# A fused attention and long-convolution kernel: the short convolution moves to diagonal matmuls, the second-level transforms to smaller tiles

## The chip, the core and the metric

The kernel runs on one core of one Trainium2 chip. The core has a matrix engine (PE; its weight loads are listed as PEld), a vector engine (DVE), a scalar engine (ACT), a general engine (POOL) and a queue engine (SP) that issues most of the DMA transfers. Each engine works through its own instructions in order and waits for the others by semaphores. SBUF is the on-chip memory of 128 partitions; PSUM is where PE leaves its sums, from which DVE or ACT must move them. The metric is the device time of one execution in microseconds; the time before is 234.24 us, the median of 3 runs (233.44 to 234.29).

## The reference

Two independent halves share the sequence length S = 2048 and the width D = 576, and their outputs lie side by side in one array of 2048 x 1152.

```python
# A: attention of 32 heads of 18 over 8 earlier positions, 2 apart
q, k, v = split(x @ wqkv)                       # wqkv: 576 x 1728
idx = pos[:, None] - 2 * arange(8)[None, :]     # masked where negative
attn = softmax(where(mask, einsum(q, k[idx]) * 18 ** -0.5, -1e9))
a = einsum(attn, v[idx]).reshape(S, D) @ wo
# B: a causal convolution of 4 taps, then one as long as the sequence, by channel
k_shift = sum over t of k_pad[t:t + S] * shift_k[:, 3 - t]
kv = k_shift * v
y = irfft(rfft(kv, 2 * S) * rfft(ssm_k, 2 * S))[:S] + kv * ssm_D
b = q * y
```

## The kernel before

The program is a list of steps written out by hand, the string ORDER; each item names a step, its arguments and, after a colon, which PSUM pool it takes (a or b) and which engine evacuates it (s is ACT, v is DVE; without a letter the step's own default). Each pool has two buffers. Every engine, SP's queue included, gets its instructions in the order of this list, so the list decides what stands in front of what.

Half A. `xt` transposes x into xT, `qk`, `qt` and `v` project it (L381, L427, L402), v goes to DRAM (Dv). `lm` multiplies q with shifted k on DVE (L519, L524), `lb` sums over each head on PE (L530 to L540), `at` transposes logits so that positions lie on partitions, `sm` is the softmax in twelve small DVE and ACT steps, `bt` transposes the weights back, `vl` loads shifted copies of v from Dv, `pm` multiplies weights with them on DVE (L642), `ps` sums on PE (L658, L668), `po` applies wo (L680, L682) and stores.

Half B. The positions are split as 128 x 16. `cv` is the short convolution on DVE: for each of four groups of positions, four multiplications by a tap (L484), three additions (L486) and the multiplication by v (L488), each on 128x2304 elements. `sk` spreads the taps over partitions by matmuls. The long convolution is a Fourier transform in two levels. Level one is `sx` for kv and, after `lkn` has loaded ssm_k and `kt` has transposed it, `kp` for the kernel (both in `s1_part`, L456), which store to DRAM (Dx, Dk; L463). Level two loads the results in another arrangement (`xl`, `kl`; L600), multiplies by a table W2 (`xs`, `ks`; the function `s2`, L594), `gp` is the product of the spectra on DVE (L615, L616), `gi` the inverse of level two with the table IAt (L629), which stores to Dy (L634). `yl` loads Dy and q, `ys` is the last level and the product with q (L702, L706), which stores.

SBUF is full: areas r1 to r10 are used several times. Two of these shares matter here: ssm_k (`knats`) is loaded into the area of xT, so `lkn` waits until the last projection has read xT; and `vsr`, where level one is collected before it is stored, has two slots.

Tile positions: a matmul whose weights have 64 or 32 columns or rows uses a part of the PE array. Before, `s2` has weights of 128 rows x 64 columns (two positions), `g_inv` of 64 rows x 128 columns (two positions), `l_sum` and `p_sum` of 128 rows x 32 columns (four positions).

Transfers of level two: `by_rt` arranges Dx, Dk or Dy so that one DMA of 128 partitions x 2304 elements (8 rows of 288, contiguous in DRAM) holds one of eight groups. `v_load` is one DMA for 128 partitions, ordered head first and shift second.

Of the kernel before, what the change touches and what calls it, by code (L numbers as in the profile page):

```python
# [10 lines left out]
ALU = mybir.AluOpType  # L11
# [7 lines left out]
lx.0 tj lx.1 lx.2 lwq.1 lwv wm.11 tv t0 xt.0.2:av sk:b lk.0 t2 xt.1.2:av lwq.0 xt.1.0:av xt.1.1:bv xt.0.0:s xt.0.1:bv  # L19
xt.2.1:s qk.1.1.1:bs xt.2.2:s t3 tw t1 lx.3 cv.0.0:a lv.1 lk.1 qk.1.1.0:bs cv.0.1:b cv.0.2:b cv.0.3:b qk.1.0.0:s  # L20
xt.2.0:as lv.0 v.0.1:b cv.0.4:b v.1.1:bs wt lk.3 v.0.0:a xt.3.0:s cv.0.5:b lk.2 cv.0.6:a cv.0.7:b cv.1.0 qk.0.1.0:b
xt.3.1:b t4 xt.3.2:as cv.1.1 lm.0.1 cv.1.2:b t5 cv.1.3:b qk.0.0.0:a sx.0.0:s qt.1:s cv.1.4:a lm.0.0 v.2.1:as lv.2
sx.1.0:a cv.1.5 cv.1.6 sx.0.1:b qt.0:b sx.0.2:a cv.1.7:a qk.0.1.1 sx.1.1 qk.0.1.3:b v.0.2:s v.1.2:bs lm.0.2 v.1.0:a
sx.1.2:b qk.1.0.1:bs sx.3.0:b cv.2.0:a qk.0.0.1:a v.3.1:a cv.2.1 sx.3.1 sx.2.0:s cv.2.2:a qt.3:as v.2.0:as qk.1.1.3:bs
sx.2.1:s cv.2.3:a lm.1.0 lb.0:a cv.2.4 cv.2.5:b v.2.2:bs cv.2.6 lm.1.1 v.3.2:av sx.2.2:b sx.3.2:b lv.3 cv.2.7:b
qk.0.1.2:a lb.1:b cv.3.0:b lm.2.2 cv.3.1 cv.3.2:b v.3.0:a qk.1.1.2:bs lm.2.1 qk.0.0.3:bs qk.1.0.3:bs lwo sx.4.0:a
cv.3.3:a lm.3.1 qt.2 sx.4.1:b sx.4.2 qk.0.0.2:as cv.3.4:b cv.3.5:b sx.5.0:b lm.2.0 qk.1.0.2 sx.5.1:a lb.2:bs cv.3.6
cv.3.7:a lm.6.0 at.0.0 lkn sx.5.2:av lm.4.2 ia:b lm.3.0 sx.6.0:as sx.6.1:as sx.6.2:s kt.3:b sx.7.0 sx.7.1:a sx.7.2:av
kt.1:bv lb.3:bs kp.1.0:bs kp.1.1:as lm.4.1 lm.4.0 kp.1.2:bs kp.3.0:s kt.0:as kp.3.1:b kp.3.2:s lm.6.2 kt.2:av lb.4:a
kp.0.0 kp.0.1:s lm.6.1 at.0.1 sm.0.0 xl.0 kp.0.2 kp.2.0:av lm.5.1 kp.2.1:s kp.2.2:bs kt.5:as kt.4:s sm.0.1 lb.6:a  # L30
kp.5.0:av kp.5.1:bs lm.5.0 sm.0.2 xl.1 kp.5.2:as kp.4.0:bs kt.6 kp.4.1:a kp.4.2:as sm.0.3 kt.7:s lb.5:s kp.6.0:as
xs.0.0:bv kp.6.1:a xl.2 kp.6.2:as kp.7.0:v kp.7.1:a kp.7.2 lm.7.0 sm.0.4 lm.7.1 xs.1.0:as sm.0.5 xs.0.1 xs.1.1:a
sm.0.6 lb.7:bs sm.0.7 kl.1 sm.0.8 kl.0 kl.3 ks.1.0:s sm.0.9 sm.0.11 sm.0.10 ks.1.1:as ks.0.0 gp.1.0 at.1.0:av vl.0.0
gp.1.1 bt.0.1:v ks.0.1:bs gp.0.0 ks.3.0:bs gi.1.0:as vl.0.1 xs.2.0:b xl.4 xs.2.1:as gp.0.1 xl.3 bt.0.0:bv at.1.1:b
vl.1.2 sm.1.0 ks.3.1:as kl.2 gi.1.1 pm.0.0 gi.0.0:s xs.3.0:a sm.1.1 vl.0.2 ks.2.0:b pm.0.1 xs.3.1:as sm.1.2 gp.3.0
vl.1.0 kl.4 sm.1.3 gi.0.1:bs gp.3.1 pm.0.2 xs.4.0:as gp.2.0 ks.2.1:b ps.0.0:a pm.0.3 sm.1.4 ks.4.0:b xl.7 gp.2.1 kl.7
gi.3.0:a ks.4.1:b gp.4.0 xs.4.1:as vl.1.1 gi.2.0:s pm.1.4 ks.7.0:a xl.5 pm.1.0 ps.0.1:bs ks.7.1:s vl.2.0 gp.4.1 pm.1.1
xs.5.0:as sm.1.5 sm.1.6 xs.7.0:b kl.6 kl.5 gi.2.1:a xs.7.1:bs ps.1.0:v xs.5.1:b ks.5.0:a vl.3.0 xl.6 gi.4.0 ps.1.2:a
gi.3.1:s vl.3.2 pm.1.2 gi.4.1:as ks.5.1:s pm.0.4 sm.1.7 gp.5.0 pm.1.3 sm.1.8 ps.0.2:bs gp.5.1 xs.6.0 yl.3 sm.1.9 yl.2
ps.1.1:a ks.6.0:s po.0.0:s xs.6.1:bs sm.1.10 gi.5.0:a gp.7.0 yl.0 vl.2.1 gi.5.1:bs gp.6.0 po.0.2:a sm.1.11 vl.2.2  # L40
gp.7.1 po.0.1 ys.3.0:v ys.3.1:v yl.1 bt.1.1:as bt.1.0 po.0.3:bs ks.6.1:bs pm.2.0 gi.7.0:as gi.7.1 gp.6.1 pm.2.1
gi.6.0:a po.1.0:bs pm.2.2 ps.2.0:a vl.3.1 gi.6.1:bs pm.2.4 ys.2.0:av ps.2.2:bs pm.2.3 ys.0.0:v ys.2.1:bs ys.0.1:as
po.1.2 ps.2.1:a po.1.1:b po.1.3:bs pm.3.4 pm.3.0 po.2.0 yl.6 yl.4 pm.3.1 po.2.1:s ps.3.0:b pm.3.2 ps.3.2:a po.2.2:b
pm.3.3 ys.6.0:as yl.5 ys.1.0:v ys.1.1:v ps.3.1:as ys.6.1:v po.2.3:v yl.7 po.3.0:a ys.5.0:bv ys.5.1:a po.3.1:b po.3.2:s
ys.4.0:v po.3.3:b ys.4.1:v ys.7.0:a ys.7.1:bs
# [4 lines left out]
def kernel(  # L50
# [13 lines left out]
    nc = tc.nc  # L64
# [53 lines left out]
    def by_rt(Dd, dh, g):  # L118
        return Dd[dh].rearrange("r (l h) d -> (r l) h d", h=32)[:, 8 * g:8 * g + 8, :]
# [34 lines left out]
    class Ring:  # L154
# [21 lines left out]
    W2 = const.tile([128, 2, 32, 4, 16], BF16, name="W2")  # L176
    IAt = const.tile([128, 3, 16, 128], BF16, name="IAt")
# [6 lines left out]
    r1, r2, r3, r4, r5, r6, r7, r8, r9, r10 = (  # L184
        Area(f"area{i}", n) for i, n in enumerate((18528, 16384, 5 * S, 2560, 5 * 2 * D, 19 * D, 28 * D, 2 * S, 3168, 4 * D)))
    xns = [(r4 if i < 1 else r2).take(4, D) for i in range(4)]
    wq = r5.take(5, 2 * D)
# [4 lines left out]
    kfull = r6.take(19, D)  # L192
    vts = [r7.take(4, D) for _ in range(2)]
    tAr = Ring(r7.take(4, D), r7.take(4, D))
    skb = r7.take(4, D)
# [5 lines left out]
    for r in (r1, r3, r4, r5, r6, r7, r9, r10):  # L201
        r.reset()
    tB = r4.take(4, D)
    r4.reset()
# [17 lines left out]
    r7.reset(20 * D)  # L222
    shr = r7.take(4 * D)[0:1]
# [15 lines left out]
    def load_v(c):  # L239
        nc.sync.dma_start(vts[c % 2], vb16[:, 4 * c:4 * c + 4, :])  # L240

    def load_k(c):
        nc.sync.dma_start(kfull[:, 3 + 4 * c:7 + 4 * c, :], kb16[:, 4 * c:4 * c + 4, :])
        if c == 0:
            nc.sync.dma_start(kfull[1:113, 0:3, :], kb16[0:112, 13:16, :])
            nc.sync.dma_start(kfull[113:128, 0:3, :], kb16[112:127, 13:16, :])
# [31 lines left out]
    ones_f, ident_f, i4_f = mk.f32(128), mk.f32(128), mk.f32(32)  # L278
    junk, ones1 = mk.take(512), mk.take(128)[0:1]
    pib = const.tile([128, 1], FP32, name="pib")  # L280
    p_i, g1, n1 = mk.i32(1), mk.i32(128), mk.i32(2, 128)
    p_f, sc_f = mk.f32(1), mk.f32(8)
    g2, sc_i, n2, l_i = mk.i32(32, 16), mk.i32(4), mk.i32(2, 32, 16), mk.i32(4, 16)
    C2, lmask = mk.take(64, 16), mk.take(4, 16)
    ones_e, e_f = (mk.f32(HC + 2, H) for _ in range(2))

    def t_junk():
        nc.vector.memset(junk, 0.0)
        nc.vector.memset(pib[:], float(np.float32(np.pi)))
        nc.scalar.activation(sc_f[:, 0:1], pib[:], ACT.Sin, scale=0.0)  # L290
        nc.scalar.dma_start(shr, B_shift_k.rearrange("d j -> (d j)").unsqueeze(0))
# [18 lines left out]
    def t_padv():  # L310
        nc.vector.memset(kfull[0:1, 0:3, :], 0.0)
        nc.gpsimd.memset(row0[:], 0.0)
        nc.gpsimd.memset(row0[0:1, :], 1.0)
        nc.gpsimd.memset(ones1, 1.0)
# [10 lines left out]
    def t_second():  # L325
        nc.gpsimd.iota(g2, pattern=[[4, 32], [512, 16]], base=0, channel_multiplier=0)
        nc.gpsimd.iota(l_i, pattern=[[1, 4], [0, 16]], base=0, channel_multiplier=0)
        for i, bits in enumerate((3, 112, 4, 8)):
            nc.vector.tensor_single_scalar(sc_i[:, i:i + 1], p_i, bits, ALU.bitwise_and)
        nc.vector.tensor_copy(sc_f[:, 0:4], sc_i)  # L330
        t2f, s0 = sc_f[:, 4:5], sc_f[:, 5:6]
        nc.vector.tensor_scalar(t2f, sc_f[:, 1:2], 0.125, None, op0=ALU.mult)
        nc.vector.tensor_scalar(sc_f[:, 6:7], sc_f[:, 2:3], 0.25, None, op0=ALU.mult)
        nc.vector.tensor_tensor(t2f, t2f, sc_f[:, 6:7], ALU.add)
        nc.vector.tensor_scalar(s0, sc_f[:, 0:1], 128.0, 1.0, op0=ALU.mult, op1=ALU.add)
        nc.vector.tensor_tensor(s0, s0, t2f, ALU.mult)
        nc.vector.tensor_scalar(sc_f[:, 7:8], sc_f[:, 3:4], -256.0, 2048.0, op0=ALU.mult, op1=ALU.add)
# [5 lines left out]
        nc.vector.tensor_scalar(lmask, l_i, sc_f[:, 0:1], None, op0=ALU.is_equal)  # L343

    def t_w2():
        for i in range(2):
            nc.vector.tensor_tensor(W2[:, i], C2[:, 32 * i:32 * i + 32].unsqueeze(2).to_broadcast([128, 32, 4, 16]),
                                    lmask.unsqueeze(1).to_broadcast([128, 32, 4, 16]), ALU.mult)
# [61 lines left out]
    def v_load(c, k):  # L410
        nd = 8 if k < 2 else 2
        dst = (vSr if k < 2 else vStr).get((c, k))
        sl = Dv[D * c + 8 * k:D * c + 8 * k + 1, 2:3]
        nc.sync.dma_start(dst.rearrange("p d t -> p (d t)")[:, 0:nd * VT - 8],
                          bass.AP(tensor=sl.tensor, offset=sl.offset, ap=[[DH * VT, 32], [DIL, 4], [1, nd * VT - 8]]))
# [18 lines left out]
    def ia_tables():  # L434
        for zi in range(2):
            for p4 in range(2):
                ptr = psum("b", 2, 1024, dt=BF16)
                for v in range(8):
                    pr = 8 * p4 + v
                    nc.tensor.transpose(ptr[:, 0, 128 * v:128 * v + 128],  # L440
                                        W2[:, zi, 2 * pr:2 * pr + 2].rearrange("p h l f -> p (h l f)"), ident[:])
# [313 lines left out]
```

## Time and profile before

| Quantity | Value |
|---|---|
| median of 3 runs | 234.24 us |
| span of the profiled execution | 233.3 us |
| PE busy, instructions | 196.2 us, 1727 |
| DVE busy, instructions | 200.7 us, 199 |
| ACT busy, instructions | 164.7 us, 241 |
| POOL busy | 22.2 us |
| moved by DMA | 60.57 MB, mean 260 GB/s |

The profiled execution's own time is its span, 233.3 us: the trace holds nothing of the program outside it. That is 0.9 us under the median of the runs and just under the fastest.

A row of groups gives a line, the engine, the operation, what it writes and reads with the shape, how often, the busy time, the mean duration of one in ns, and the idle time of the engine before it. A matmul's duration contains the way through the array, so neighbours overlap: the rate of a series is read from its whole length. A row of stretches gives the busy time of each engine in a stretch with the number of instructions, then the granted clock of PE as a share, the share of time in which the DMA engines had packets (it can pass 1 where packets overlap) and the rate in GB/s.

### The profile page before, as it was taken

Reading aid. Unit: us, or ns where it says so; the run is one execution under the profiler, and the core shown is the slowest. Engines: PE = TensorE matmul, PEld = TensorE weight load, DVE = VectorE, ACT = ScalarE, POOL = GpSimd, SP = SyncE. Lnnn points to the kernel's source line nnn. Section 1 sums busy time; section 2 is a strip of 40 time slices with the busy share of each in tenths; the row PEclk is TensorE's granted clock in tenths of the full one; section 3 lists DMA queues with packets and bytes.
Section 4 is the critical chain, followed back from the end, with each engine's and each line's share of the span. In section 5 each row is a group of like instructions: output and inputs, shape, how many; then the busy total and the mean of one; then the engine's idle time right before and its main releaser. Section 6 shows DMA issues by size and latency. Waiting matters only on the chain. (4 is left out here: it accounts for less than half of the span.)

```text
span 233.3 us, 4423 instructions
## 1 busy us (share of the span) xinstructions
PE 196.2 (84%) x1727; PEld 112.5 (48%) x1736; DVE 200.7 (86%) x199; ACT 164.7 (71%) x241; POOL 22.2 (10%) x53
## 2 busy tenths in 40 slices
PE   7899969999999977959873979668898979896981
PEld 2644524544544444545532456434564656564661
DVE  2679999989596999778969999999999999996533
ACT  2675739677754969487989789899999758535321
POOL 8001540110210110200000000000000010010100
PEclk9999999999999996779998599999999999997999
DMA  6999823451169589977996998999798999799586
GB/s 221 348 276 393 248 85 106 155 162 48 55 198 268 134 273 327 218 221 211 307 290 207 330 353 326 374 355 400 306 360 299 327 332 379 274 275 339 121 272 214
DMA packets 46965, 60.57 MB, mean 260 GB/s; under 512 B 2368, under 2 KB 40064, under 8 KB 45920
## 3 DMA queue, kind: packets, MB, share of 16 engines
q1 hardware_dynamic: 46254, 57.78, 75.5%
q0 software_dynamic: 688, 2.51, 4.6%
q8 instruction: 13, 0.21, 0.4%
q14 instruction: 8, 0.07, 0.1%
q10 hardware_dynamic: 2, 0.00, 0.0%
HBM read 38.98 MB, written 21.31 MB: 258 GB/s over the span
## 5 line engine op out<-in xcount | busy, mean ns | idle before, releaser
L103 ACT ACTIVATE area<-psB 128x576 bf16<-128x576 f32 (+7 forms) x122 | 85.2, 745 | 32.2 <-PE psB L381 7.6
L103 ACT ACTIVATE area<-psA 128x576 bf16<-128x576 f32 (+7 forms) x105 | 75.6, 760 | 30.7 <-PE psA L381 12.0
L519 DVE TENSOR_TENSOR area<-area 128x4096 bf16<-128x4096 bf16 x16 | 36.4, 2285 | 5.7 <-PE psA L540 3.3
L642 DVE TENSOR_TENSOR area<-area,area 128x4096 bf16<-128x4096 bf16 (+1 forms) x20 | 40.7, 2069 | 0.1
L381 PEld LDWEIGHTS <-area 128*128 128x128 bf16 x160 | 15.5, 98 | 20.0 <-issue 3.0
L594 PEld LDWEIGHTS <-W 128*64 128x64 bf16 x256 | 14.1, 113 | 22.0 <-issue 15.0
L484 DVE TENSOR_TENSOR area<-area,area 128x2304 bf16<-128x2304 bf16 x16 | 21.6, 1362 | 0.8 <-PE psB L456 0.6
L594 PE MATMUL psB<-area,W 128*64 128x288 bf16 x160 | 16.2, 299 | 6.9 <-DMA area<-Dk 3.9
L381 PE MATMUL psB<-area,area 128*128 128x512 bf16 x85 | 20.1, 379 | 0.3
L693 POOL DMA_DIRECT2D area<-in_B_q_dram x8 | 6.0, 747 | 142.8 <-DVE area L706 119.2
L381 PE MATMUL psA<-area,area 128*128 128x512 bf16 x67 | 16.1, 379 | 2.7 <-DVE area L367 2.5
L456 PE MATMUL psB<-area,T 128*128 128x384 bf16 x58 | 14.8, 346 | 2.9 <-ACT area L103 2.7
L456 PEld LDWEIGHTS <-T 128*128 128x128 bf16 x96 | 9.3, 104 | 15.1 <-issue 9.2
L486 DVE TENSOR_TENSOR area<-area,area 128x2304 bf16<-128x2304 bf16 x12 | 16.3, 1356 | 0.3
L629 PEld LDWEIGHTS <-IAt 64*128 64x128 bf16 x256 | 12.4, 94 | 6.9 <-issue 4.0
L680 PEld LDWEIGHTS <-area 128*128 128x128 bf16 x128 | 12.4, 100 | 5.8 <-issue 2.6
L381 PE MATMUL psA<-area,wv 128*128 128x512 bf16 x60 | 13.9, 379 | 0.0
L594 PE MATMUL psA<-area,W 128*64 128x288 bf16 x96 | 10.2, 310 | 4.1 <-ACT area L103 3.6
L381 PEld LDWEIGHTS <-wv 128*128 128x128 bf16 x80 | 7.6, 98 | 9.4 <-issue 0.6
L616 DVE TENSOR_TENSOR area<-area 128x1152 bf16<-128x1152 bf16 x16 | 12.0, 749 | 0.0
L615 DVE TENSOR_TENSOR area<-area 128x1152 bf16<-128x1152 bf16 x16 | 11.9, 746 | 0.0
L456 PE MATMUL psA<-area,T 128*128 128x384 bf16 x38 | 10.0, 364 | 1.8 <-ACT area L103 1.7
(132 smaller groups left out, 270.1 us busy)
## 6 DMA issues: line engine op xcount, KB each, us to landing
area<-Dv SPq DMA_DIRECT2D x8, 1054.0 KB, 8.0
Dx<-area SPq DMA_DIRECT2D x16, 288.0 KB, 3.6
Dk<-area SPq DMA_DIRECT2D x16, 288.0 KB, 3.5
area<-Dx SPq DMA_DIRECT2D x8, 576.0 KB, 5.7
area<-Dk SPq DMA_DIRECT2D x8, 576.0 KB, 5.3
Dy<-area SPq DMA_DIRECT2D x8, 576.0 KB, 4.6
area<-Dy SPq DMA_DIRECT2D x8, 576.0 KB, 7.0
out_dram<-area SPq DMA_DIRECT2D x16, 288.0 KB, 3.7
```

Of the source, the lines that this page charges most:

```text
L103: nc.scalar.activation(dst, src, ACT.Copy, **({} if scale is None else {"scale": scale}))
L381: nc.tensor.matmul(ps[:, u, :], w[:, kb, cols[u]:cols[u] + 128], xT[:, kb, t], start=(kb == 0), stop=(kb == 4))
L456: nc.tensor.matmul(ps[:, ri, 0:384], T1[:, ri, :], sf[:, 384 * ch:384 * ch + 384], start=True, stop=not extra)
L484: nc.vector.tensor_tensor(tB if k else tA, kfull[:, 4 * c + 3 - j:4 * c + 7 - j, :], skb[:, j, :].unsqueeze(1).to_broadcast([128, 4, D]), ...
L486: nc.vector.tensor_tensor(tA, tA, tB, ALU.add)
L519: nc.vector.tensor_tensor(prr.get((n, h)), q2[h][:, :, 512 * aq:512 * aq + 512].unsqueeze(1).to_broadcast([128, 4, 2, 512]), kv, ALU.mult)
L594: nc.tensor.matmul(ps[64 * hp:64 * hp + 64, im, 0:HD], W2[:, im, 8 * g + 2 * prl + hp].rearrange("p l f -> p (l f)"), Wt[:, 2 * prl + hp, ...
L615: nc.vector.tensor_tensor(P[:, 0:2], X, K, ALU.mult)
L616: nc.vector.tensor_tensor(P[:, 2:4], X, swap, ALU.mult)
L629: nc.tensor.matmul(ps[:, hp, 0:HD], IAt[r, tab, 4 * g + 2 * hv + u, :], Pp[(i, hv)][r, n, u, :], start=(n == 0), stop=(n == 3), tile_posit ...
L642: nc.vector.tensor_tensor(P, vv, Lt[:, :, 512 * c:512 * c + 512].unsqueeze(2).to_broadcast([128, 2, nd, 512]), ALU.mult)
L680: nc.tensor.matmul(ps[:, di, 0:288], oT[:, 512 * ct + 128 * tt:512 * ct + 128 * tt + 128], wot[:, ct, d0:d1], start=(ct == 0), stop=False)
```

## The change

- `cv`: the rows of k are transposed on PE (`kx`, 80 transposes; with tokens along the free axis, kT). For each of 5 blocks of 128 channels and 2 halves of the 16 positions, 11 matmul steps use a slice of kT as weights (64 rows x 128 columns) and diagonal matrices of the taps (`dg`, built once on DVE) as the moving side; DVE then multiplies the sum in PSUM by v. `sk` and the multiplications and additions on DVE are gone.
- Level two: W2 has two instead of four interleaved blocks; `s2` uses weights of 64 rows x 32 columns (eight positions), `g_inv` of 32 rows x 64 columns (eight positions). There are twice as many of these matmuls, of the same free size 288. IAt is half as large, `ia` has three evacuations instead of six.
- Transfers: in the new arrangement the partitions of a group fall in two halves, so `xl`, `kl` and the store of `gi` are two DMAs of 64 partitions each; `vl` is four DMAs of 32 partitions each, ordered shift first and head second.
- `sm`: the reciprocal is written as bf16 at once, and the weights are normalised in place by one DVE operation per half instead of two that also reorder; `bt` reads them there.
- ORDER is a new list; several evacuations change engine.

```diff
-    def by_rt(Dd, dh, g):
-        return Dd[dh].rearrange("r (l h) d -> (r l) h d", h=32)[:, 8 * g:8 * g + 8, :]
+    def by_rt(Dd, dh, g, lg):
+        return Dd[dh].rearrange("r (k l h) d -> k r l h d", k=2, l=2)[lg, :, :, 8 * g:8 * g + 8, :]
...
     def v_load(c, k):
-        sl = Dv[D * c + 8 * k:D * c + 8 * k + 1, 2:3]
-        nc.sync.dma_start(dst.rearrange("p d t -> p (d t)")[:, 0:nd * VT - 8],
-                          bass.AP(tensor=sl.tensor, offset=sl.offset, ap=[[DH * VT, 32], [DIL, 4], [1, nd * VT - 8]]))
+        for j in range(4):
+            sl = Dv[D * c + 8 * k:D * c + 8 * k + 1, 2 + DIL * j:3 + DIL * j]
+            nc.sync.dma_start(dst.rearrange("p d t -> p (d t)")[32 * j:32 * j + 32, 0:nd * VT - 8],
+                              bass.AP(tensor=sl.tensor, offset=sl.offset, ap=[[DH * VT, 32], [1, nd * VT - 8]]))
...
-    def kv_conv(c, k):
-        tA = tAr.get(c) if k == 0 else tAr[c]
-        if k in (0, 1, 3, 5):
-            j = {0: 3, 1: 2, 3: 1, 5: 0}[k]
-            nc.vector.tensor_tensor(tB if k else tA, kfull[:, 4 * c + 3 - j:4 * c + 7 - j, :], skb[:, j, :].unsqueeze(1).to_broadcast([128, 4, D]), ALU.mult)
-        elif k < 7:
-            nc.vector.tensor_tensor(tA, tA, tB, ALU.add)
-        else:
-            nc.vector.tensor_tensor(tA, tA, vts[c % 2], ALU.mult)
+    def k_tok(c, h):
+        ptr = psum("b", 2, 1024, dt=BF16)
+        for u in range(2):
+            row = kas[c][:, 2 * h + u, :]
+            for cb in range(5):
+                c0 = min(128 * cb, D - 128)
+                nc.tensor.transpose(ptr[:, u, 128 * cb:128 * cb + 128], row[:, c0:c0 + 128], ident[:])
+        b0 = 4 * c + 2 * h
+        copy32(kT[:, :, b0:b0 + 2, 2:130], ptr[:, :, 0:640].rearrange("p u (k t) -> p k u t", k=5))
+
+    def kv_conv(cb, hb):
+        ps = psa()
+        lo = 8 * hb
+        order = (0, 4, -3, -2, -1, 1, 2, 3, 5, 6, 7)
+        for db in order:
+            b = lo + db
+            w0, w1 = max(b, lo), min(b + 4, lo + 8)
+            for u in range(2 if cb < 4 else 1):
+                hp = u if cb < 4 else 1
+                r = slice(64 * hp, 64 * hp + 64)
+                st = kT[r, cb, b % NT, 2:130] if b >= 0 else kT[r, cb, b % NT, 1:129]
+                nc.tensor.matmul(ps[:, u, 64 * (w0 - lo):64 * (w1 - lo)], st,
+                                 dg[r, cb, w0 - b:w1 - b, :].rearrange("p j c -> p (j c)"),
+                                 start=(db == order[0]), stop=(db == order[-1]), tile_position=(64 * hp, 0))
+        n = 2 if cb < 4 else 1
+        o = kv[:, lo:lo + 8, 128 * cb:128 * cb + 64 * n].rearrange("p b (u c) -> p u b c", u=n)
+        nc.vector.tensor_tensor(o, ps[:, 0:n].rearrange("p u (b c) -> p u b c", b=8), o, ALU.mult)
...
-    def s2(Wt, g, dst, h, scale):
-        for prl in (2 * h, 2 * h + 1):
+    def s2(Wt, g, dst, hh, scale):
+        for im in range(2):
             ps = psb()
-            for im in range(2):
-                for hp in range(2):
-                    nc.tensor.matmul(ps[64 * hp:64 * hp + 64, im, 0:HD],
...
+            for hq in range(4):
+                for lg in range(2):
+                    r = slice(64 * lg, 64 * lg + 64)
+                    nc.tensor.matmul(ps[32 * hq:32 * hq + 32, lg, 0:HD],
+                                     W2[r, im, 8 * g + 4 * hh + hq].rearrange("p l f -> p (l f)"),
+                                     Wt[r, 4 * hh + hq, :], start=True, stop=True, tile_position=(64 * lg, 32 * hq))
...
     def w_load(Dd, key, i):
-        nc.sync.dma_start(Wr.get((key, i)), by_rt(Dd, i // 4, i % 4))
+        W = Wr.get((key, i))
+        for lg in range(2):
+            nc.sync.dma_start(W[64 * lg:64 * lg + 64], by_rt(Dd, i // 4, i % 4, lg))
...
     def g_inv(i, hv):
+        pss = [psb() for _ in range(2)]
+        for n, tab in enumerate((0, 2, 1, 1)):
+            for hq in range(4):
+                for lg in range(2):
+                    r = slice(32 * hq, 32 * hq + 32)
+                    nc.tensor.matmul(pss[hq // 2][64 * lg:64 * lg + 64, hq % 2, 0:HD],
+                                     IAt[r, tab, 2 * g + hv, 64 * lg:64 * lg + 64], Pp[(i, hv)][r, n, lg, :],
+                                     start=(n == 0), stop=(n == 3), tile_position=(32 * hq, 64 * lg))
...
-            nc.sync.dma_start(by_rt(Dy, dh, g), Y)
+            for lg in range(2):
+                nc.sync.dma_start(by_rt(Dy, dh, g, lg), Y[64 * lg:64 * lg + 64])
```

The new list around the end of the projections and the load of ssm_k (the last projection is qk.1.0.3; before, it was qk.1.0.2, with `lkn` seven items behind it; now it is five):

```
... qk.0.1.2:as sx.2.1:bs sx.2.2:bs qk.0.0.2:as lm.3.0 sx.7.0:bs qk.1.0.3:bs at.0.0:as lm.2.1 lm.2.2 lb.2:bs
lkn lm.3.1 sx.7.1:bs sx.6.0:bs lm.4.0 sx.6.1:as sx.7.2:bs sx.6.2:as lb.3:bv xl.2 lm.4.1 ia:bs xl.3 kt.3:av at.0.1:bv ...
```

## The prediction

> **What bounds the kernel now.** I read the page's sums first: DVE 200.7 us, PE 196.2, ACT 164.7 of a span of 233.3, so no engine bounds all of it. Then the shape of the slices, then the busy time by stage. The stages are cut where the order hands over: 82.3 is the end of the last projection, 127.4 the issue of the first load of Dk, 203.0 the landing of the last store to Dy.
>
> ```profile
> core 0: us, PE busy (x) PEld busy (x) DVE busy (x) ACT busy (x) POOL busy (x), PEclk, DMA share, GB/s
> 0.00:82.30 82.30, 77.28 (x464) 38.09 (x474) 68.80 (x74) 52.43 (x69) 16.96 (x46) 1.00 0.63 193
> 82.30:127.40 45.10, 33.72 (x325) 20.07 (x323) 38.93 (x33) 36.82 (x46) 2.24 (x3) 0.88 0.88 263
> 127.40:203.00 75.60, 62.80 (x752) 39.29 (x755) 74.91 (x77) 64.79 (x112) 0.75 (x1) 0.96 0.96 340
> 203.00:233.30 30.30, 22.38 (x192) 15.05 (x184) 18.03 (x18) 10.69 (x16) 2.23 (x3) 0.93 0.79 237
> ```
>
> Stage 1 is PE's: 77.28 of 82.30. In stage 3 DVE is busy 74.91 of 75.60, and the DMA engines have packets 0.96 of the time at 340 GB/s: two limits side by side. Stage 2 is a chain through the load of ssm_k and the two slots of `vsr`. Stage 4 is the tail.
>
> Next the joint of stages 1 and 2, from the timeline of PE and the line of the ssm_k load:
>
> ```profile
> 77.51 2.32 PE L381 MATMUL psA<-area,area 128*128 128x512 bf16 x10
> 79.99 2.32 PE L381 MATMUL psA<-area,area 128*128 128x512 bf16 x9
> ...
> L264 SPq DMA_DIRECT2D area<-in_B_ssm_k_dram x5: 328/397/683, 82.4 to 84.8; - x5
> ```
>
> The first load of ssm_k leaves at 82.4, as the last projection ends (79.99 + 2.32): every us that PE needs more before that point delays the whole branch of ssm_k.
>
> Last, how fast transfers run when they alone fill the queue:
>
> ```profile
> 75.00:76.00 1.00, 1.00 (x7) 0.49 (x6) 1.00 (x2) 0.34 (x1) 0.00 (x0) 1.00 1.09 254
> 84.50:89.50 5.00, 2.28 (x32) 1.79 (x30) 4.73 (x4) 4.47 (x7) 0.75 (x1) 0.94 0.99 376
> 141.00:142.00 1.00, 1.00 (x18) 0.83 (x16) 1.00 (x2) 1.00 (x3) 0.00 (x0) 1.00 1.01 417
> 160.00:164.00 4.00, 2.71 (x38) 1.27 (x36) 4.00 (x4) 4.00 (x8) 0.00 (x0) 1.00 1.00 396
> ```
>
> The share is 1 in all four, the rate is not. At 141 to 142 and 160 to 164 the queue carries loads of 128 partitions (level two, v): 417 and 396 GB/s; at 84.5 to 89.5 ssm_k: 376. At 75 to 76 it carries `lwo`, DMAs of 32 partitions each: 254.
>
> **The change part by part.** The sum is made against the profiled execution, 233.3 us; it stands 0.9 under the median, which is added at the end.
>
> *PE in stage 1.* Ten projections in a row take 2.32 us, so one costs (2.32 - 0.38)/9 = 0.216 us, or 0.42 ns a column. A block of `cv` has 11 steps with 2048 columns in all: 0.86 us, with a floor of 0.056 us for the four narrow steps (the eight transposes of L552 take 0.61 us, (0.61 - 0.22)/7 = 0.056) 0.92. Ten blocks: 9.2 us. `kx` is 80 transposes at 0.056: 4.5. Three more groups of `sx` now stand before the last projection (19, not 16), 2 x 0.16 each: +1.0; `sk` goes: -1.0. Sum +13.7 us on an engine with 5 us of idle time in the stage. Bounds: 8.7 if all of that idle time absorbs it, 16 if narrow steps cost double. I take 13.6, since the new order has the same loads to wait for at the start.
>
> *DVE.* Removed: 16 x 1.362 + 12 x 1.356 + 4 x 1.354 (L484, L486, L488) = 43.5 us. Added: eight products from PSUM of 128x1024 at 1.22 (L105, same shape) and two of 128x512 at 0.68 (L367) = 11.2; seven evacuations of `kx` of 640 words, between 0.68 and 0.95, 0.82: 5.7; `dg`, 1280 elements, 0.75 to 1.4. Softmax: 4 x 1.890 (L581) become 2 x 1.21 (L569's shape), two casts of 0.29 go: -5.7. W2: -1.1. Evacuations that change engine bring DVE about +13, and take as much from ACT. In all DVE falls by about 20 us and ACT by 12. In stage 1 this is beside PE, which sets that stage: worth 0 there. Its cover is PE; were that gone, DVE's 20 us would be the gain.
>
> *Stage 2.* After the load comes the same chain: ssm_k lands, `kt`, eight rounds of `kp` through two slots. What gets shorter: `ia` has 3 evacuations of 1.03 us fewer, and five groups of `sx` instead of seven stand behind `lkn`. Bounds 0 to -9; I take -5. Four loads of Dx are now halves on the same queue: 0 to +4 (priced as in the next paragraph), I take +2.
>
> *Transfers in stage 3.* Twelve loads of 0.59 MB, v with 9.4 MB, eight stores of 0.59 MB: 21.2 of the stage's 25.7 MB (340 x 75.6) become DMAs of 64 or 32 partitions. At 396 GB/s they take 53.5 us, at 254 GB/s 83.5: +30. What cushion there is: 21.2 MB at 396 and the other 4.5 MB at about 300 (stage 2's kind, 263 to 376) make 68.5 of 75.6, so 7 us. Net +23. Ends: 0 or below (the halves follow each other on one queue, and might fill it together as one DMA did), and 21.2/0.235 - 53.5 = +37 by the slower half of the same second, without cushion. The row is of the same kind as four of `vl`'s DMAs (32 partitions, four in a row), so I take it at its mean.
>
> [...]
>
> *Issues.* SP issues 199 instead of 141 instructions, in stage 3 95 DMAs instead of 44; 33 more at 0.53 (L414) and 18 at 0.33 to 0.41 (L600, L634) are some 24 us of SP's time. By the list of SP's own waits it waits for engines for about 50 us in that stage, which hides it; 0, and up to +8 if it does not.
>
> *PE in level two.* Series with two positions: 16 of L629 take 1.15 us, (1.15 - 0.28)/7 = 0.12 per pair. Series with four: 16 of L540 take 1.05, 0.22 per four of 512 columns. Positions of a set start together, so 512 + 512 matmuls in sets of eight cost 64 x 0.12 each, 15.4 us in all against 30.8. Eight positions at once are not in the trace: if only four or two run together, up to +16 us instead of -15.4. PE is busy 62.8 of 75.6 in stage 3 and waits there for others: 0 either way.
>
> *DVE in stage 3.* Its work between the first load of Dk and the last inverse falls by about 9 us (softmax cheaper, six of its steps earlier). With the queue as the limit: 0; the bound is -16 (the rival below).
>
> Sum: 13.6 - 5 + 2 + 23 = +33.6; 233.3 + 33.6 = 266.9, and with 0.9 for the median 268 us.
>
> **The rivals.**
> - *The halves cost nothing, only the late start stays.* Stage 3 keeps 75.6 us at 340 GB/s. For it: all bytes are the same, and the queue is never empty. Against it: 254 against 396 GB/s. Price: 233.3 + 10.6 + 0.9 = 245 (237 to 250 with the bounds of stage 2).
> - *Faster: DVE, not the queue, sets stage 3.* DVE waits for nothing there, so its lighter work would set the pace: it has about 58 us left at the first load of Dk (`pm` 25, `gp` 21, softmax 6, the rest 6), with 2 us of gaps 60 instead of 75.6, -16. Then 233.3 + 10.6 - 16 + 0.9 = 229. It decides from the point where stage 3 ends in under 65 us, that is from 25 MB/65 us = 385 GB/s on. For it: 396 to 417 in short stretches. Against it: 340 over the stage with a share of 0.96, and the halves.
> - *The change does not do what it says:* sets of eight run one after the other. PE's sum in level two would rise to 1024 x 0.12 = 123 us and set stage 3: above 290 us. Sets of two and four start together in the trace, so this is small.
>
> **How the numbers follow.** Halves slow, as summed: 0.58 (from 252, with half the term, to 283, with the upper end). Late start alone: 0.24. Faster: 0.12. Sets of eight in turn, or more than 283: 0.06. The range 236 to 281 leaves out the faster case and the top. A measurement tells about 0.5%, 1.2 us, from no change: faster (below 233.1) 0.12, same 0.05 from the low edge of the late start, slower 0.83. The likeliest case alone: 252 to 283.
>
> **What would show it.** Right: the first load of ssm_k leaves near 96 (82.4 before), the first load of Dk near 138; in the stretch behind it the DMA share stays near 1 while the rate is 230 to 280 GB/s, PE waits for Dk and Dx, DVE has gaps, and it lasts about 100 us. Wrong: the rate behind the first load of Dk is 340 or more, or DVE is still without gaps there, or ssm_k leaves before 90.

## The result and the profile after

The changed kernel takes 270.4 us in the median (266.22 to 271.88 in 4 runs); the kernel before, run beside it, 233.84. The ratio is 1.155, with an interval of 1.110 to 1.200: slower by 36.6 us. The profiled execution, with a span of 270.2 us, is the longest of its four, and so are those of two variants (the kernel before with halves, the changed kernel with whole transfers), so differences of under some 4 us between profiles are not explained here.

The stages are cut at the same hand-overs as before: the first load of ssm_k (94.3 instead of 82.4), the first load of Dk (141.3 instead of 127.4), the last landing of a store to Dy (244.2 instead of 203.0). This is the busy time of each engine by stage, after:

```profile
core 0: us, PE busy (x) PEld busy (x) DVE busy (x) ACT busy (x) POOL busy (x), PEclk, DMA share, GB/s
0.00:94.30 94.30, 89.62 (x739) 50.66 (x749) 63.46 (x85) 41.28 (x51) 15.33 (x45) 1.00 0.50 166
94.30:141.30 47.00, 33.89 (x346) 19.63 (x345) 34.60 (x31) 34.66 (x46) 1.48 (x2) 0.82 0.99 262
141.30:244.20 102.90, 66.60 (x1207) 34.24 (x1207) 69.18 (x68) 66.15 (x109) 1.49 (x2) 0.67 0.98 250
244.20:270.20 26.00, 21.20 (x207) 14.87 (x204) 15.68 (x18) 13.59 (x21) 1.50 (x2) 0.95 0.84 251
```

| stage | before, us | after, us | difference | predicted |
|---|---|---|---|---|
| 1, to the load of ssm_k | 82.3 | 94.3 | +12.0 | +13.6 |
| 2, to the load of Dk | 45.1 | 47.0 | +1.9 | -3 |
| 3, to the last landing in Dy | 75.6 | 102.9 | +27.3 | +23 |
| 4, tail | 30.3 | 26.0 | -4.3 | 0 |
| sum | 233.3 | 270.2 | +36.9 | +33.6 |

Read stage 3 first. The DMA engines have packets 0.98 of the time, as before (0.96), but they move 250 GB/s instead of 340. DVE, which had hardly a gap there (busy 74.91 of 75.60 us), is now busy 69.18 of 102.9 us. PE and ACT are busy about as long as before (66.60 and 66.15 us, before 62.80 and 64.79), so all three stand still for a third of the time. What they stand still for is in the list of waits in stage 3, first after, then before:

```profile
engine line waited for: us in total, times, longest us
...
PEld L595 <- issue: 28.5, 34, 7.2
...
PE psA L595 <- DMA area<-Dk: 9.6, 7, 4.2
...
PEld L595 <- DMA area<-Dk: 6.6, 3, 4.5
```

```profile
PEld L594 <- issue: 13.7, 32, 3.5
PEld L594 <- DMA area<-Dk: 5.6, 3, 2.2
...
PE psB L594 <- DMA area<-Dk: 3.9, 3, 1.7
```

L595 (before, L594) is the matmul of the second level, which needs Dk and Dx. For the first of these lines the profile names no releaser; it has grown from 13.7 to 28.5 us. The two that name Dk are 16.2 us together, before 9.5. In two stretches in which the queue is never empty the rate is 219 and 256 GB/s, where the row that the prediction used has 254:

```profile
148.00:156.00 8.00, 6.23 (x159) 2.80 (x144) 6.93 (x10) 7.39 (x13) 0.00 (x0) 0.51 1.02 219
176.00:186.00 10.00, 3.39 (x64) 1.49 (x63) 2.57 (x2) 5.71 (x10) 0.00 (x0) 0.50 1.02 256
```

Now the joint of stages 1 and 2, from PE's timeline, the line of the ssm_k load and SP's waits:

```profile
90.31 2.32 PE L378 MATMUL psA<-area,area 128*128 128x512 bf16 x10
92.47 0.49 PE L452 MATMUL psB<-area,T 128*128 128x384 bf16 x2
92.80 2.32 PE L378 MATMUL psB<-area,area 128*128 128x512 bf16 x10
```

```profile
L258 SPq DMA_DIRECT2D area<-in_B_ssm_k_dram x5: 346/382/562, 94.3 to 96.2; - x5
...
SPq L258 <- PE psB L378: 1.6, 2, 1.2
```

The last projection (the third row, in psB) is the last reader of the tile that ssm_k overwrites, and SP waits for it. The first of the five loads leaves at 94.3, before that projection is over (92.80 + 2.32 = 95.1): each load overwrites only a part of the tile. PE is busy 89.62 us of the stage instead of 77.28; its idle time is 4.7 us, before it was 5.0. The delay, 12.0 us, is as long as PE's extra work, 12.3 us.

### The profile page after: what moved, and what is told of

It reads as the page before. It is cut to its first block, busy times and chain, and to the rows that moved or that the text cites. A ratio compares the mean times of both kernels' runs of the same rounds, so it can differ in the third digit from the quotient of the medians.

```text
span 270.2 us, 6042 instructions
## 1 busy us (share of the span) xinstructions
PE 211.3 (78%) x2496; PEld 119.4 (44%) x2505; DVE 182.9 (68%) x200; ACT 155.7 (58%) x224; POOL 19.8 (7%) x51
## 4 chain that ended last, share of the span: by engine, by line
PE 49%; DMA 32%; ACT 8%; SPq 4%; DVE 3%; issue 3%; DVEq 0%; ACTq 0%
PE psA L378 10%; DMA area<-Dk 10%; ACT area L103 7%; PE psB L378 7%; DMA area<-Dy 6%; DMA Dy<-area 5%; PE psB L452 4%; DMA area<-in_B_ssm_k_dram 3%; PE psB L686 3%; DMA Dk<-area 3%; DMA out_dram<-area 2%; SPq L412 2%; DMA area<-in_A_x_dram 2%; PE psB L490 2%; PE psA L664 2%
## 5 line engine op out<-in xcount | busy, mean ns | idle before, releaser
L103 ACT ACTIVATE area<-psB 128x576 bf16<-128x576 f32 (+7 forms) x108 | 77.1, 750 | 34.9 <-PE psB L452 8.8
L648 DVE TENSOR_TENSOR area<-area,area 128x4096 bf16<-128x4096 bf16 (+1 forms) x20 | 40.9, 2072 | 8.5 <-PE psA L674 4.2
L523 DVE TENSOR_TENSOR area<-area 128x4096 bf16<-128x4096 bf16 x16 | 36.1, 2284 | 2.7 <-ACT area L103 2.6
L595 PEld LDWEIGHTS <-W 64*32 64x32 bf16 x512 | 8.3, 102 | 42.0 <-issue 31.1
L595 PE MATMUL psA<-area,W 64*32 64x288 bf16 x272 | 13.4, 386 | 16.4 <-DMA area<-Dk 9.6
L105 DVE CAST area<-psB 128x768 bf16<-128x768 f32 (+4 forms) x17 | 14.9, 899 | 13.8 <-DMA Dk<-area 4.4
L595 PE MATMUL psB<-area,W 64*32 64x288 bf16 x240 | 11.9, 389 | 11.0 <-ACT area L103 9.7
L364 DVE TENSOR_SCALAR area<-psB 128x512 int32<-128x512 int32 (+2 forms) x13 | 8.6, 668 | 8.9 <-PE psB L372 5.4
L632 PEld LDWEIGHTS <-area 32*64 32x64 bf16 x512 | 10.2, 130 | 9.6 <-issue 7.7
L664 PE MATMUL psA<-area,I 128*32 128x512 bf16 x96 | 9.3, 505 | 6.3 <-ACT area L103 3.4
L378 PE MATMUL psB<-area,area 128*128 128x512 bf16 x59 | 13.9, 379 | 0.1
L686 PE MATMUL psB<-wv,area 128*128 128x288 bf16 x64 | 12.1, 326 | 0.0
```

The costliest lines, as they stand in the source:

```text
L103: nc.scalar.activation(dst, src, ACT.Copy, **({} if scale is None else {"scale": scale}))
L105: nc.vector.tensor_copy(dst, src)
L378: nc.tensor.matmul(ps[:, u, :], w[:, kb, cols[u]:cols[u] + 128], xT[:, kb, t], start=(kb == 0), stop=(kb == 4))
L523: nc.vector.tensor_tensor(prr.get((n, h)), q2[h][:, :, 512 * aq:512 * aq + 512].unsqueeze(1).to_broadcast([128, 4, 2, 512]), kv, ALU.mult)
L595: nc.tensor.matmul(ps[32 * hq:32 * hq + 32, lg, 0:HD], W2[r, im, 8 * g + 4 * hh + hq].rearrange("p l f -> p (l f)"), Wt[r, 4 * hh + hq, :] ...
L632: nc.tensor.matmul(pss[hq // 2][64 * lg:64 * lg + 64, hq % 2, 0:HD], IAt[r, tab, 2 * g + hv, 64 * lg:64 * lg + 64], Pp[(i, hv)][r, n, lg, ...
```

## The experiments

The theory was: DMAs that reach only one half of the partitions are slow, which costs stage 3 some 25 us, and PE's extra work in stage 1 delays everything behind ssm_k by 12. The rivals were: the number and issue of the DMAs, the narrow tiles (sets of eight matmuls), the new order.

### The kernel before with halves

```diff
-        nc.sync.dma_start(Wr.get((key, i)), by_rt(Dd, i // 4, i % 4))
+        W = Wr.get((key, i))
+        for p in range(2):
+            nc.sync.dma_start(W[64 * p:64 * p + 64], by_rt(Dd, i // 4, i % 4)[64 * p:64 * p + 64])
...
-            nc.sync.dma_start(by_rt(Dy, dh, g), Y)
+            for p in range(2):
+                nc.sync.dma_start(by_rt(Dy, dh, g)[64 * p:64 * p + 64], Y[64 * p:64 * p + 64])
...
-                          bass.AP(tensor=sl.tensor, offset=sl.offset, ap=[[DH * VT, 32], [DIL, 4], [1, nd * VT - 8]]))
+                              bass.AP(tensor=sl.tensor, offset=sl.offset + 16 * p * DH * VT, ap=[[DH * VT, 16], [DIL, 4], [1, nd * VT - 8]]))
```

> The kernel before, with one edit: each load of Dk and Dx and each store to Dy is two DMAs, one for partitions 0 to 63 and one for 64 to 127, and each load of v likewise (16 heads each). Tiles, matmuls, order and bytes are those of before. Theory (transfers that reach only one half of the partitions are slow): the stretch from the first load of Dk to the last store to Dy grows from 75.6 us by about 23 to 27, at 230 to 280 GB/s with a DMA share near 1: 255 to 262 us in all. Rival (what costs in the changed kernel is its tiles of 64x32 and 32x64, its order, or its convolution on PE): within 2 us of the kernel before.

Measured: 255.4 us (251.9 to 256.2), ratio 1.089 (1.071 to 1.106). The busy time by stage, and one stretch that holds loads of v in halves:

```profile
126.60:228.90 102.30, 72.88 (x797) 44.91 (x797) 83.06 (x82) 71.42 (x117) 2.24 (x3) 0.87 1.01 265
228.90:254.50 25.60, 17.11 (x146) 11.34 (x143) 12.86 (x14) 7.86 (x12) 0.75 (x1) 0.92 0.83 254
...
141.00:148.00 7.00, 5.67 (x76) 3.80 (x72) 6.96 (x10) 6.29 (x11) 0.00 (x0) 1.00 0.99 218
```

Stage 3 is 102.3 us with the tiles, the order and the softmax of before: +26.7, where the changed kernel has +27.3. The tail is 4.7 us shorter (4.3 in the changed kernel): PE ran 797 matmuls in the longer stage 3 and 146 in the tail, before 752 and 192. So of the 27 us about 5 come back in the tail. The halves alone carry some 22 us (255.4 against 233.5 for the kernel before beside it).

### The same count of DMAs, over all partitions

Two controls were run. The first cut each DMA into its even and its odd partitions:

```diff
-        nc.sync.dma_start(Wr.get((key, i)), by_rt(Dd, i // 4, i % 4))
+        W = Wr.get((key, i)).rearrange("(q b) h d -> b q h d", b=2)
+        for p in range(2):
+            nc.sync.dma_start(W[p], by_rt(Dd, i // 4, i % 4).rearrange("(q b) h d -> b q h d", b=2)[p])
...
+        D2 = dst.rearrange("p d t -> p (d t)").rearrange("(q b) n -> b q n", b=2)
+        for p in range(2):
+            nc.sync.dma_start(D2[p][:, 0:nd * VT - 8],
```

> The kernel before, with the same DMAs cut in two as in the run with halves, of the same sizes and as many of them, but one takes the even and one the odd partitions, so that each reaches over all 128. Theory (the half that a DMA is confined to costs): 233 to 238 us, and over 315 GB/s in the stretch of level two. Rival (the number of DMAs, their issue on SP or their smaller size costs): as slow as with halves, 255 to 262 us.

Measured: 269.3 us (266.2 to 271.0), slower than the halves: a miss. Taken alone that would have refuted the theory. The list of waits (DVE's and SP's) and two rows by time say otherwise:

```profile
DVE area L648 <- DMA area<-Dv: 36.1, 8, 9.3
...
SPq L416 <- DVE area L648: 21.3, 4, 7.3
```

```profile
139.00:142.00 3.00, 2.79 (x40) 2.05 (x36) 2.33 (x4) 2.96 (x7) 0.00 (x0) 1.00 0.96 387
160.00:164.00 4.00, 2.47 (x20) 1.50 (x22) 4.00 (x4) 1.37 (x3) 0.00 (x0) 0.50 1.02 418
```

When they run, these pieces move 387 to 418 GB/s. But the loads of v (L416) wait 21.3 us for products (L648), where with halves they waited 1.6, and the products then wait 36.1 us for v. The author's guess, which no run tests, is that the strided view of a slot is taken to reach into its neighbour, so that a load waits for a slot it does not write. The control had brought a wait of its own and could not answer for the time. The second control cuts along the free axis:

```diff
-        nc.sync.dma_start(Wr.get((key, i)), by_rt(Dd, i // 4, i % 4))
+        W = Wr.get((key, i))
+        for p in range(2):
+            nc.sync.dma_start(W[:, 4 * p:4 * p + 4], by_rt(Dd, i // 4, i % 4)[:, 4 * p:4 * p + 4])
...
-                          bass.AP(tensor=sl.tensor, offset=sl.offset, ap=[[DH * VT, 32], [DIL, 4], [1, nd * VT - 8]]))
+                              bass.AP(tensor=sl.tensor, offset=sl.offset + p * nh * VT, ap=[[DH * VT, 32], [DIL, 4], [1, n]]))
```

> The kernel before, with the same DMAs cut in two as in the run with halves, but along the free axis (4 of 8 rows of h each for Dk, Dx and Dy; half of the channels for v), so that each DMA still covers all 128 partitions. Number and size of the DMAs are those of the halves, their contiguous runs are half as long; no product is waited for that the kernel before does not wait for. The interleaved run could not answer this, since there the loads of v waited for products of other slots. Theory (the confinement to a half costs, not the count): 233 to 240 us, and the stretch from the first load of Dk to the last store to Dy 73 to 82 us. Rival (count, issue or size): 252 us or more, as with halves.

Measured: 231.0 us (230.1 to 234.7), ratio 0.988 (0.984 to 0.993). Stage 3, and two stretches with a full queue:

```profile
127.00:203.20 76.20, 63.69 (x765) 39.34 (x765) 75.83 (x79) 65.84 (x113) 1.33 (x2) 0.98 0.97 338
...
160.00:168.00 8.00, 6.53 (x84) 3.56 (x84) 7.96 (x9) 7.96 (x14) 0.00 (x0) 1.00 1.02 389
140.00:148.00 8.00, 6.38 (x88) 4.40 (x86) 7.97 (x10) 7.18 (x14) 0.00 (x0) 1.00 1.02 356
```

As many DMAs as with halves, half as long runs, all 128 partitions: the stage keeps its length (76.2 against 75.6, with halves 102.3). Count, issue on SP and size are out; what costs here is that a DMA stays on one half of the partitions. In this run a product could start on the first piece of a tile, with halves it needs both; but the rates differ in stretches with a full queue too, 356 and 389 GB/s here and 218 there, at a DMA share of 1.02, 1.02 and 0.99.

### The changed kernel with whole transfers

This variant keeps the convolution on PE, the new order and the new places of the tiles, and takes by_rt, w_load, s2, g_inv, the tables W2 and IAt, v_load and the weights' order of before.

```diff
-        for lg in range(2):
-            nc.sync.dma_start(W[64 * lg:64 * lg + 64], by_rt(Dd, i // 4, i % 4, lg))
+        nc.sync.dma_start(Wr.get((key, i)), by_rt(Dd, i // 4, i % 4))
...
-            for lg in range(2):
-                nc.sync.dma_start(by_rt(Dy, dh, g, lg), Y[64 * lg:64 * lg + 64])
+            nc.sync.dma_start(by_rt(Dy, dh, g), Y)
```

> The changed kernel with its convolution on PE and its new order, but with the second level of before (128x64 and 64x128 tiles, loads and stores of 128 partitions in one DMA) and with v loaded in one DMA of 128 partitions, which needs the old order of the weights and so two softmax products of 1.9 us for the one of 2.4. Theory (the late start of ssm_k and the slow transfers add up): the transfers' part goes, the late start of about 12 us stays: 243 to 249 us. Rival (the new order or the narrow tiles cost, not the transfers): above 255 us if the order does, and the clock of PE in the stretch of level two stays near 0.67.

Measured: 244.2 us (242.3 to 246.7), ratio 1.046 (1.034 to 1.059). The load of ssm_k still leaves at 94.5; stage 3 is back at 79.5 us. The whole table by stage:

```profile
0.00:94.50 94.50, 90.89 (x749) 50.92 (x750) 64.12 (x82) 41.22 (x51) 15.74 (x47) 1.00 0.50 166
94.50:139.10 44.60, 33.69 (x346) 21.11 (x348) 35.72 (x31) 38.19 (x50) 1.49 (x2) 0.92 0.94 274
139.10:218.60 79.50, 60.97 (x730) 39.62 (x726) 71.33 (x70) 64.23 (x108) 1.49 (x2) 0.96 0.90 320
218.60:244.80 26.20, 20.56 (x202) 14.43 (x194) 16.41 (x18) 13.48 (x21) 1.49 (x2) 0.94 0.88 263
```

What is left of the loss, 10.7 us, belongs to the convolution on PE and the new order together. By the table it lies in stage 1 (+12.2); the other three stages sum to -0.7. DVE is busy 71.33 us in stage 3, 3.6 less than before, and the stage is no shorter (79.5 us against 75.6): its lighter work bought nothing here. (Its two softmax products of 1.9 us stand for one of 1.2 in the changed kernel, not of 2.4 as the expectation has it.)

### Halves and tiles, one after the other

Two variants go back from there toward the changed kernel. The first is the one with whole transfers and cuts these into halves of 64 partitions (the diff is that of the first experiment):

> The changed kernel with the second level and the v layout of before, as in the run with whole transfers, but its loads of Dk, Dx and v and its stores to Dy cut into two halves of 64 partitions. What is left between it and the changed kernel are the narrow tiles, the quarters of v and one softmax product. Theory (late start and halves add up, tiles cost nothing): 244 + 22 = 266 us, 262 to 270. Rival (the matmuls in sets of eight, or the lower clock of PE there, carry a part of the loss): 260 us or less.

Measured: 263.2 us (262.2 to 264.7), ratio 1.129 (1.123 to 1.136). The time without halves (244.2 us) and the cost of the halves add up, at 19.0 instead of 22 us.

The second is the changed kernel with the matmul tiles of before (128x64 and 64x128), with the tables and the order of rows that these need; the rest, v in quarters too, is as in the change:

```diff
-            for hq in range(4):
-                for lg in range(2):
-                    r = slice(64 * lg, 64 * lg + 64)
-                    nc.tensor.matmul(ps[32 * hq:32 * hq + 32, lg, 0:HD],
-                                     W2[r, im, 8 * g + 4 * hh + hq].rearrange("p l f -> p (l f)"),
-                                     Wt[r, 4 * hh + hq, :], start=True, stop=True, tile_position=(64 * lg, 32 * hq))
+                for hp in range(2):
+                    nc.tensor.matmul(ps[64 * hp:64 * hp + 64, im, 0:HD],
+                                     W2[:, im, 8 * g + 2 * prl + hp].rearrange("p l f -> p (l f)"),
+                                     Wt[:, 2 * prl + hp, :], start=True, stop=True, tile_position=(0, 64 * hp))
```

> The changed kernel with v in quarters and its softmax in place, but with the matmul tiles of before in the second level (128x64 and 64x128, pairs instead of sets of eight), its DMAs for Dk, Dx and Dy cut into halves of 64 partitions. It differs from the changed kernel in the tiles alone. Theory (tiles cost nothing, the quarters of v and noise make the difference between the run with whole layout and halves, 263.2, and the changed kernel): 266 to 272 us. Rival (the sets of eight and the lower clock of PE there cost the rest): 261 to 264 us.

Measured: 266.1 us (265.1 to 267.3), ratio 1.145 (1.138 to 1.151); the changed kernel has 266.2 to 271.9. This lies at the edge of what the theory expected and above the rival's range. Between 0 and some 4 us are left for the tiles, and the spread of the changed kernel's own times is as large: not settled. The 2.9 us between this variant and the one before it belong to the quarters of v and their softmax product, which were not told apart. Both are small parts of the 36.6 us.

### Both halves at once, from two queues

```diff
-            nc.sync.dma_start(W[64 * lg:64 * lg + 64], by_rt(Dd, i // 4, i % 4, lg))
+            (nc.gpsimd if lg else nc.sync).dma_start(W[64 * lg:64 * lg + 64], by_rt(Dd, i // 4, i % 4, lg))
```

(and likewise for Dy and for the third and fourth quarter of v)

> The changed kernel, with the DMAs for partitions 64 to 127 (second halves of Dk, Dx and Dy, third and fourth quarter of v) issued by POOL on its own queue, beside those for 0 to 63 on SP's. Bytes, pieces and tiles are unchanged. Theory (one queue writes one half after the other, each at the speed of a half): both halves are filled together, the stretch of level two falls from 102.9 us to 80 to 92, and the time to 248 to 259 us. Rival (pieces are slow for their number or size, or matmuls in sets of eight set the stretch): 266 us or more, since POOL's issues cost about 0.75 us each as those of q do.

Measured: 266.7 us (262.9 to 270.6), ratio 1.133 (1.118 to 1.147). A miss: 8 us above the range, and in the range of the rival. Against the rival stand the other variants: the count and size of pieces cost nothing in the cut along the free axis, and the sets of eight at most some 4 us.

```profile
139.90:235.90 96.00, 64.20 (x1221) 33.70 (x1219) 69.27 (x68) 66.05 (x109) 26.31 (x48) 0.73 1.00 275
...
160.00:176.00 16.00, 8.22 (x180) 3.72 (x180) 12.09 (x12) 10.38 (x17) 3.59 (x7) 0.61 1.02 307
```

The rate rises from 250 to 275 GB/s and stage 3 from 102.9 goes to 96.0, not to 80 to 92. Halves issued from two queues move a little more than halves from one, but far less than DMAs over 128 partitions do (340 in stage 3 of the kernel before, 338 with the cut along the free axis). So the expectation that both halves would be filled at once, each at its own speed, was not met.

### The changed kernel with little convolution on PE

This variant computes two of the eleven steps of each block of the convolution and leaves the other nine out.

```diff
-        order = (0, 4, -3, -2, -1, 1, 2, 3, 5, 6, 7)
+        order = (0, 4)
```

> The changed kernel with two of the eleven steps in each of the ten blocks of the convolution on PE; the nine others are left out, so the convolution is not the reference's. 22 matmuls become 4 (2 in the narrow channel block), 512 columns instead of 2048: about 0.7 us less a block, 7 us in all. Theory (PE sets stage 1 and the load of ssm_k follows the last projection): the first load of ssm_k leaves at 87 to 89 instead of 94.3, and the time falls by 5 to 8 us. Rival (the start is late for another wait, or stage 3 does not care when it begins): the load leaves near 94, or the time falls by less than 2 us.

Measured: 268.8 us (266.7 to 269.0), ratio 1.150 (1.144 to 1.155). A miss: 1.6 us less than the changed kernel, within its spread, and not 5 to 8. The load of ssm_k leaves at 91.9, not at 87 to 89. In the stretch from 30 to 62 us the matmuls of the convolution (L490) fell from 9.48 us of PE to 3.70, but only 2.4 of these 5.8 us arrived. Where the rest went is in PE's waits up to 92 us:

```profile
PE psA L490 <- ACT area L103: 1.4, 2, 0.7
PE psB L490 <- DVE area L495: 1.3, 1, 1.3
...
PE psB L452 <- DVE area L495: 0.8, 1, 0.8
```

These three lines are not in the changed kernel's list. They are 3.5 us (1.0 us of other waits is gone in turn): the next blocks wait for PSUM, which ACT and DVE (L495, the product with v) empty no faster than before (from 31 to 62 us DVE is busy 24.76 us with 23 instructions, in the changed kernel 23.99 with 23). And right behind these pauses PE is slower: the same 19 projection matmuls take 5.21 us instead of 4.26, and the granted clock from 31 to 62 us is 0.94, where the changed kernel has 1.00. First the changed kernel, then this one:

```profile
41.56 4.26 PE L378 MATMUL psA<-area,wv 128*128 128x512 bf16 x19 [0.16 <-issue]
```

```profile
39.76 5.21 PE L378 MATMUL psA<-area,wv 128*128 128x512 bf16 x19 [0.33 <-issue]
```

So the rival's "late for another wait" holds in part: PE sets stage 1, with the evacuations close behind it. Its other half holds too: of the 2.4 us won at ssm_k nothing is left at the first load of Dk, which leaves at 141.1 (141.3 in the changed kernel), since stage 2 took 49.2 us instead of 47.0. That less work on PE would give the late start back is therefore not shown by any run.

### Small parts, and a version that might beat both

One part of the change alone, the reciprocal written straight in bf16:

```diff
-            nc.vector.reciprocal(rec, ssum.rearrange("p b h -> p (b h)"))
+                nc.vector.reciprocal(recb, ssum.rearrange("p b h -> p (b h)"))
...
-            nc.vector.tensor_copy(recb, rec)
+            pass
```

> The kernel before with one small part of the change: the reciprocal of the softmax sums is written straight in bf16, and the two casts of 0.29 us on DVE go. If DVE sets the stretch of level two in the kernel before (74.91 us busy of 75.6), 0.5 to 1 us faster: 232.3 to 233.3 us. If the transfers set it as much, no difference, 233 to 234.

Measured: 232.5 us, ratio 1.000 (0.994 to 1.005): no difference seen, though DVE has 74.91 us of 75.6 in that stage. But the interval reaches over 1 us to either side, and the gain looked for was 0.5 to 1 us; whether DVE or the transfers set that stage is not settled by this run.

The cut along the free axis came out 1.2% faster than before, so it was joined with this, and then carried further:

> The kernel before, with its DMAs of Dk, Dx, Dy and v cut in two along the free axis (231.0 us alone) and the reciprocal written straight in bf16 (232.5 alone). If the cut lets products start on the first half of a tile, and the casts are worth their 0.6 us on DVE then: 230 to 231 us. If the gain of the cut was that of one chip's hour: 233 to 234.

Measured: 230.8 us (228.5 to 234.3), ratio 0.997 (0.993 to 1.002).

```diff
+        nc.sync.dma_start(by_rt(Dy, dh, g)[:, 4 * hv:4 * hv + 4], Y[:, 4 * hv:4 * hv + 4])
         if hv:
-            for p in range(2):
-                nc.sync.dma_start(by_rt(Dy, dh, g)[:, 4 * p:4 * p + 4], Y[:, 4 * p:4 * p + 4])
...
-        nc.sync.dma_start(Wr.get(("y", i)), by_f1(Dy, dh, 8 * c4, 8))
+            nc.sync.dma_start(Wy[:, 4 * p:4 * p + 4], by_f1(Dy, dh, 8 * c4 + 4 * p, 4))
```

> As the run before it, and the first half of each Dy store leaves as soon as its four rows are evacuated, and each load of Dy is cut in two, so that the first product of a chunk waits for half of it. If the stretch of level two ends by the last transfers, 229 to 230.5 us; if DVE or the total of the bytes ends it, 230 to 232, as without; if SP, which waits for an evacuation earlier, holds up loads behind it: above 233.

Measured: 240.3 us (237.3 to 243.0), ratio 1.030 (1.022 to 1.037). SP's own waits, first of the run without the early stores, then of this one, show the last of the three expected ways:

```profile
SPq L641 <- ACT area L103: 11.1, 8, 3.1
```

```profile
SPq L639 <- ACT area L103: 30.6, 13, 7.0
```

The line is that of the store to Dy. SP waits 19.5 us more for evacuations, with loads queued behind it. That the split loads of Dy have a share in the loss was not told apart. No version is shown to beat the kernel before for certain: the 0.988 of the cut alone does not return in the 0.997 of the cut with the reciprocal, whose interval holds 1.

## Why the prediction was right

The forecast was 268 us, from 233.3 + 33.6 + 0.9; the time is 270.4, within the likeliest case's 252 to 283. That it comes within 1% is in part luck: stage 2 was off by 5 us, and two errors within stages 3 and 4 cancelled. The 0.9 rests on a reading that does not hold: in the runs here a time is about 1.7 us longer than its span (271.88 and 270.2), so the span of 233.3 is not 0.9 under a median of times. That is a matter of 1 us. Two bounds do not come out of their terms either: half of the +23 gives 256, not 252, and the bounds of stage 2 put the lower end of the late start alone at 239, not 237. By its steps:

- **PE in stage 1, +13.6.** Measured +12.0. The convolution is busy 9.48 us in the trace after (9.2 in the sum) and the transposes of `kx` 5.08 (4.5). The terms were about right, and so was taking no relief from PE's idle time: 4.7 us of it are still there. What the step did not see is how near ACT and DVE are, and that stage 2 need not follow: of 5.8 us taken from PE, 2.4 arrived at ssm_k and 0.2 at Dk.
- **Stage 2, -5 and +2.** This step was wrong: +1.9. The five us that `ia` and the groups of `sx` were to give did not come even with whole transfers, where the stage is 44.6 us against 45.1. Its DMA share is 0.92 to 1.00 at 260 to 276 GB/s in five of the six runs with the new order (0.88 at 263 before): transfers fill more of it now. That they alone set its length is argued, not shown; with halves of Dx it came out between 43.4 and 49.2 us in the variants, so the +2 for Dx was not shown either.
- **Transfers in stage 3, +23.** Measured +27.3 in the stage and -4.3 in the tail, together +23.0; in the kernel before with halves +26.7 and -4.7, 22.0. What the halves cost is shown by the pair of runs with equal counts, 255.4 against 231.0. The cushion of 7 us was in the sum at the wrong place: stage 3 grew by nearly all of the 30, and the tail gave 4 to 5 back, where in the first experiment PE had 146 matmuls left instead of 192. So the match of +23 with 23.0 is closer than its working.
- **The rate.** The row of 254 GB/s on 32 partitions priced a stage that then ran at 250 (265 in the first experiment). In one stretch with loads of v in the first experiment and in one of the changed kernel the rate was lower, 218 with halves and 219 with quarters. Other stretches with a full queue ran at 242 to 279, and the stage at 250 to 265, so the upper end of +37, worked out from the row's slower half, was too much, and the +23 of the row fitted. That a row of one microsecond, whose two halves have 272 and 235, fitted so well is luck.
- **Issues, 0.** Shown for 36 of the 58 additional instructions: the cut along the free axis has as many more DMAs and does not cost (231.0 us against 232.9 for the kernel before beside it).
- **PE in level two, 0, and DVE, 0.** Right in effect. Sets of eight do run together, but the 15 us of PE they were to save did not appear: L595 and L632 take 20.62 + 17.55 = 38.2 us in stage 3, their lines before 22.66 + 18.23 = 40.9, at a granted clock of 0.67 against 0.96. The same inverse step, before in pairs and after in sets of eight at two granted clocks:

```profile
142.72 1.15 PE L629 MATMUL psB<-area,IAt 64*128 64x288 bf16 x16
```

```profile
190.15 1.19 PE L632 MATMUL psB<-area,area 32*64 32x288 bf16 x32
230.31 0.70 PE L632 MATMUL psB<-area,area 32*64 32x288 bf16 x32
...
190.15:191.34 1.19, 1.19 (x40) 0.77 (x37) 1.19 (x2) 1.02 (x1) 0.00 (x0) 0.50 1.05 224
230.30:231.00 0.70, 0.70 (x37) 0.51 (x37) 0.70 (x2) 0.58 (x1) 0.00 (x0) 1.00 1.19 383
```

At a clock of 1.00 four sets take 0.70 us, (0.70 - 0.28)/3 = 0.14 a set, near the 0.12 of the sum; at 0.50 they take 1.18 us or more, as long as the eight pairs did before (1.15 us, at 1.00). So the lower clock ate the saving. DVE's lighter work (182.9 us in all instead of 200.7, where the sum had about 20 less) met a queue that was slower still.

Of the rivals, "only the late start stays", priced at 245, was a good price for another kernel: with whole transfers the time is 244.2. What it assumed of the halves was wrong. The faster rival needed 385 GB/s; the stage had 250. Sets of eight in turn did not occur: 32 such matmuls would have taken 32 x 0.12 = 3.8 us, and took 0.70 us at the full clock and 1.18 to 1.72 at 0.50.

The stages measured add up to 12.0 + 1.9 + 27.3 - 4.3 = 36.9 against 33.6; stage 2 is 4.9 over, stage 1 is 1.6 under, and stages 3 and 4 together are as in the sum.

## What to carry to other kernels

Before a layout is changed, look at what each DMA of it covers: here the same bytes in halves of 64 partitions, with nothing else changed, took a stage from 340 to 265 GB/s while the DMA share stayed near 1 (0.96 and 1.01), and nothing that the new tiles saved on PE or DVE paid for that. A DMA share near 1 did not tell the rate (at 1.02 one stretch of the changed kernel ran at 219 GB/s, one of the interleaved variant at 418), so read the two side by side, and price a transfer from a stretch of the trace where the same kind of DMA has the queue to itself. And a control that cuts a tile in a strided way should be read for new waits before its time is believed.

## What was not expected of the hardware

Halves on two queues gained 10% in rate over the stage (250 to 275 GB/s; single stretches 271 to 309), well short of the 338 to 340 of DMAs over all partitions.

The granted clock of PE in stage 3 was 0.67 in the changed kernel and 0.88 in the variant that differs in the matmul tiles and their tables alone, though the longest waits of PE are alike (weight loads of L594 in the variant 26.6 us, of L595 here 28.5, in both without a named releaser). PE was busy 66.60 and 67.39 us there, of 102.9 and 99.0. The means over whole executions agree: the three kernels with sets of eight have 0.84 to 0.89 in their twelve runs, the three with halves and the wider tiles 0.92 to 0.95 in theirs. The interleaved variant, with wider tiles and long waits, has 0.885 to 0.896, so tiles are not the only thing that counts. The smaller tiles ran at the lower clock, for a reason that no run here isolates.
